# An attention, gated MLP and token-mixing kernel on one core: the written-out order of its 3395 operations is replaced by another

## The chip, the cores and the metric

One core of a Trainium2 chip runs one program. The time is the device time of one execution in microseconds (us). The engines are TensorE (PE in the profile; PEld is its loading of weights), VectorE (DVE), ScalarE (ACT), GpSimd (POOL) and SyncE (SP), and 16 DMA engines that all queues share. A DMA is issued by SP, by POOL or, at the very start, by ACT, and counts as an instruction of that queue: an issue stands in the queue behind whatever the issuing engine waits for.

## What is computed

Three blocks in a row, all float32, with 4 batches, 448 positions, 768 features (12 heads of 64):

```python
scores = cap * np.tanh(scale * (q @ k.T) / cap)          # per batch and head
attn = exp(scores) / sum(exp(scores))
x = concat_heads(attn @ v)                                # (4, 448, 768)

h = relu(x @ w_in)                                        # d_ff 1024: u | v
v_n = (v - mean) / sqrt(var + 1e-6)
v_s = einsum('ts,bsd->btd', w_spatial, v_n) + b_spatial
x = (u * v_s) @ w_out

theta = x @ w_theta
y = einsum('ts,bsd->btd', w_tok_r, x * cos(theta)) + einsum('ts,bsd->btd', w_tok_i, x * sin(theta))
u = x + y
out = u + relu(u @ w_ch)
```

The MLP weights come as 64-bit words and are turned into float32 on the chip.

## The kernel before

Most products are made three times, from the high and low parts of both factors, which are float32 values rounded to a coarser form and the differences left over. In the scores the two parts lie over each other in the partitions, so that one pass of 128 rows does two of these products.

**Attention** runs over pairs of heads. The six pairs of the first batch are "direct": their probabilities go into the product with V unsplit (`attend_1`, L833). All the rest, three batches of six pairs, splits the probabilities (`attend`). For a pair, in turn:

- SP, ACT or POOL loads Q, K and V. Pairs 0 and 1 load each Q half by itself (`load_twice` L568, the tails of 64 rows L571 and L576, `load_k` L536); the others load Q and K for two pairs at once (`load_q` L529, L536, `load_tails` L543). V of a direct pair comes by four small DMAs (`load_v1`, L619 and L621), into one of two buffers, whose ones and zeros POOL sets by five memsets at the start (`ones_1`, L462 to L466).
- PE turns Q and K (`turn`: L642 to L646 for pairs 0 and 1, L659 for others) into a PSUM tile `tqk`.
- ACT and DVE copy the high parts of Q (`y`, L683) and K (`XA` L713, `XB` L714), DVE makes the low ones (L359, the helper `difference`). POOL copies pieces of K to where each product needs them (`XT`, L719, L721, L723; `XH`, L730).
- From pair 2 on, Q's high part is needed in both halves of the partitions. This is done by DMAs from SBUF to SBUF on SP, 112 KB each: `y_odd` (L706, two DMAs) fills the tile `y1` from `y0`, then `y_even` (L709) writes the upper half of `y0` once y_odd has read it and DVE has made the low part from it. The tiles are called `y` for even and `Y` for odd pairs among the direct ones, and `yl` holds the low part.
- PE makes four groups of scores (L356, the helper `products`; one of 3 and three of 4 products), ACT takes tanh (L769) and exp (L772) of each, and PE adds up the products with V in `acc` (L356). Copies of `acc` and its row sums follow (L859, L867); a gather of the sums through DRAM (L924, L928, L935, L940) and the division end the pair.

Beside this, in the first 100 us, POOL and SP load w_in in twelve DMAs of 512 KB (`load`, L986), and POOL, ACT and DVE turn each into float32 and into high and low parts (L399 to L420, L999, L359); the turning of w_spatial (L1037 to L1062) follows.

**The rest**: v, u and the spatial mix of the MLP for each batch (`moe1_v`, `moe1_u`, `moe1_s`), the second product, theta with cos and sin, the token mix, the last product with w_ch. Attention of one batch runs between MLP work of the batch before it.

**What sets the order.** Each step is entered in a list by `op(...)` with its engine, its readers and writers, but it is emitted only at the end, in the sequence of a table of numbers, `ORDER` (L47 to L217). `Plan.order` returns the table, and the last lines of the kernel go through it:

```python
    def order(self):

        assert sorted(ORDER) == list(range(len(self.ops)))
        place = {i: n for n, i in enumerate(ORDER)}
        assert all(place[d] < place[i] for i, op in enumerate(self.ops) for d in op[4])
        return ORDER
...
    with tc.manual_schedule():
        for i in plan.order():
            plan.ops[i][3]()
```

Each engine executes its own instructions in the sequence in which they were emitted; a step waits in its queue until what it reads is there and what it overwrites is free, and everything behind it in that queue waits too.

Of the kernel before, what the change touches and what calls it, by code (L numbers as in the profile page):

```python
# [47 lines left out]
    4, 9, 10, 5, 7, 8, 2, 36, 12, 38, 3, 6, 0, 11, 31, 33, 35, 13, 1, 14, 34, 37, 32, 15, 29, 16, 195, 27, 18, 23, 20,  # L48
    30, 26, 17, 21, 56, 28, 19, 22, 39, 24, 25, 140, 70, 63, 143, 141, 142, 40, 144, 145, 57, 58, 146, 54, 52, 196,
    41, 53, 149, 147, 48, 55, 194, 45, 51, 43, 71, 148, 59, 154, 46, 42, 72, 150, 155, 64, 44, 65, 156, 47, 153, 60,  # L50
    49, 151, 66, 50, 161, 152, 198, 61, 162, 67, 77, 163, 164, 73, 62, 200, 157, 210, 202, 165, 212, 211, 74, 199,
    207, 167, 166, 197, 201, 175, 208, 159, 168, 204, 206, 170, 79, 205, 176, 203, 78, 160, 169, 236, 68, 213, 80, 84,
    158, 171, 286, 248, 209, 81, 238, 69, 177, 249, 174, 173, 237, 285, 172, 240, 82, 287, 239, 241, 217, 243, 83, 86,
    250, 214, 218, 178, 242, 215, 98, 247, 219, 244, 245, 220, 85, 180, 235, 216, 246, 87, 228, 179, 91, 221, 223, 75,
    88, 229, 76, 181, 222, 251, 289, 105, 230, 224, 89, 100, 90, 301, 291, 302, 303, 227, 290, 226, 99, 296, 293, 225,
    299, 292, 294, 182, 298, 231, 297, 101, 295, 93, 92, 252, 102, 232, 288, 255, 106, 300, 253, 331, 233, 256, 103,
    107, 258, 104, 254, 304, 183, 108, 266, 257, 119, 471, 259, 261, 472, 94, 267, 109, 260, 95, 110, 305, 126, 343,
    265, 184, 96, 268, 344, 345, 111, 121, 120, 262, 333, 234, 97, 332, 112, 122, 473, 308, 306, 338, 263, 269, 335,
    309, 340, 123, 336, 307, 264, 372, 311, 124, 310, 334, 339, 319, 271, 337, 312, 346, 125, 128, 314, 272, 270, 330,
    313, 341, 114, 373, 127, 315, 113, 129, 320, 342, 185, 318, 115, 321, 374, 130, 316, 322, 116, 376, 273, 317, 133,  # L60
    131, 347, 324, 377, 350, 348, 325, 475, 323, 353, 378, 351, 132, 354, 361, 379, 349, 478, 274, 474, 186, 352, 117,
    380, 187, 383, 188, 118, 381, 356, 275, 490, 189, 191, 492, 384, 355, 192, 190, 479, 357, 375, 193, 480, 276, 362,
    483, 491, 489, 382, 488, 134, 360, 485, 482, 358, 487, 493, 486, 363, 385, 476, 326, 386, 477, 389, 481, 327, 364,
    359, 387, 328, 390, 484, 525, 278, 329, 494, 365, 277, 526, 282, 501, 388, 495, 283, 279, 392, 496, 280, 284, 506,
    502, 366, 497, 393, 391, 281, 507, 498, 512, 527, 367, 503, 529, 528, 508, 404, 582, 394, 541, 584, 509, 504, 395,
    542, 513, 396, 543, 368, 405, 505, 499, 531, 583, 514, 406, 510, 511, 530, 539, 369, 585, 407, 500, 515, 537, 517,
    516, 534, 408, 544, 518, 520, 532, 538, 533, 540, 521, 535, 536, 135, 370, 136, 522, 397, 371, 519, 586, 545, 398,
    137, 587, 552, 546, 523, 409, 547, 399, 524, 553, 557, 138, 635, 416, 550, 554, 139, 563, 551, 558, 417, 548, 555,
    588, 410, 556, 418, 400, 600, 419, 559, 602, 601, 562, 564, 549, 560, 401, 420, 590, 565, 428, 598, 429, 589, 561,
    430, 566, 595, 431, 603, 421, 567, 593, 568, 422, 591, 571, 569, 596, 592, 594, 597, 572, 570, 599, 402, 411, 604,  # L70
    573, 636, 403, 611, 412, 605, 432, 574, 606, 616, 423, 612, 575, 609, 413, 433, 637, 617, 622, 610, 613, 638, 424,
    694, 443, 623, 414, 444, 614, 607, 445, 425, 650, 691, 446, 624, 652, 447, 615, 448, 618, 608, 692, 621, 434, 651,
    619, 449, 435, 639, 457, 620, 625, 693, 646, 450, 640, 415, 451, 436, 643, 576, 630, 626, 653, 647, 627, 642, 631,
    645, 628, 641, 648, 649, 629, 644, 452, 437, 632, 695, 654, 633, 696, 661, 426, 655, 634, 453, 656, 438, 745, 577,
    427, 666, 662, 659, 454, 667, 439, 672, 578, 657, 663, 697, 660, 668, 458, 658, 459, 709, 669, 440, 460, 664, 711,
    461, 673, 665, 455, 579, 698, 462, 674, 670, 702, 671, 456, 710, 705, 463, 677, 700, 708, 675, 712, 441, 703, 680,
    699, 676, 678, 707, 464, 701, 465, 704, 679, 706, 681, 442, 581, 713, 580, 682, 746, 796, 819, 683, 714, 720, 820,
    747, 684, 816, 821, 725, 715, 817, 721, 797, 718, 916, 798, 726, 731, 716, 719, 722, 748, 685, 732, 717, 799, 818,
    466, 800, 760, 913, 467, 723, 761, 762, 806, 727, 724, 807, 914, 808, 733, 728, 686, 730, 749, 729, 750, 756, 687,
    809, 734, 468, 915, 752, 755, 751, 739, 753, 757, 735, 758, 763, 736, 810, 740, 754, 738, 759, 688, 737, 834, 742,  # L80
    917, 469, 743, 918, 741, 764, 470, 835, 765, 966, 771, 766, 801, 769, 772, 744, 776, 770, 773, 767, 802, 689, 803,
    777, 804, 690, 782, 774, 768, 919, 778, 805, 775, 811, 931, 779, 812, 783, 933, 932, 813, 921, 814, 780, 920, 928,
    781, 784, 815, 927, 822, 787, 922, 924, 785, 929, 823, 925, 790, 825, 786, 934, 926, 828, 836, 824, 788, 826, 846,
    930, 791, 789, 827, 923, 837, 829, 792, 967, 830, 935, 793, 968, 838, 794, 936, 942, 937, 1025, 947, 940, 943,
    847, 948, 941, 848, 944, 795, 849, 938, 953, 831, 939, 945, 969, 832, 954, 946, 850, 833, 1022, 839, 981, 949,
    982, 983, 952, 840, 950, 1023, 970, 851, 841, 955, 974, 858, 980, 951, 977, 971, 859, 852, 1024, 972, 860, 956,
    978, 973, 976, 961, 975, 853, 979, 984, 842, 958, 957, 854, 861, 959, 843, 962, 960, 862, 963, 1026, 844, 985,
    1027, 964, 992, 986, 845, 965, 863, 987, 1075, 993, 997, 990, 855, 870, 864, 1003, 998, 991, 988, 856, 885, 994,
    1028, 989, 999, 871, 865, 872, 1040, 857, 1000, 873, 995, 1042, 1041, 886, 1004, 887, 996, 866, 888, 1030, 874,
    1029, 1001, 1005, 1002, 1033, 875, 1006, 1032, 1043, 1008, 1036, 1031, 1037, 876, 1038, 1007, 1011, 1034, 1009,  # L90
    889, 1010, 1039, 1012, 877, 1035, 867, 878, 1044, 868, 1013, 1076, 879, 890, 1045, 1014, 1077, 1051, 1046, 869,
    1015, 1056, 891, 1049, 1134, 1052, 899, 1057, 892, 880, 1050, 893, 1053, 1016, 1047, 1078, 881, 1058, 1062, 1132,
    1048, 1054, 894, 1059, 882, 895, 1090, 1063, 896, 1092, 1091, 897, 1060, 1064, 900, 1133, 901, 1079, 1055, 898,
    1070, 1086, 1131, 1080, 1017, 883, 1018, 1085, 1061, 1081, 1089, 1082, 1087, 1067, 1084, 1065, 1093, 1083, 884,
    1088, 902, 1066, 1068, 903, 904, 1069, 1019, 1071, 905, 1094, 1073, 1135, 1101, 1095, 1136, 1074, 1072, 906, 1102,
    1106, 1185, 1096, 1112, 1107, 1099, 1020, 907, 1097, 1103, 1137, 1100, 908, 1113, 909, 1098, 1149, 1021, 910,
    1104, 1151, 1150, 911, 1108, 1105, 1236, 1237, 1138, 1109, 1114, 1111, 1140, 1142, 1110, 1139, 1145, 1238, 912,
    1115, 1239, 1141, 1152, 1117, 1146, 1240, 1256, 1148, 1143, 1116, 1259, 1147, 1120, 1118, 1119, 1121, 1144, 1260,
    1257, 1153, 1261, 1122, 1186, 1160, 1258, 1123, 1154, 1187, 1124, 1241, 1155, 1165, 1161, 1158, 1356, 1242, 1159,
    1166, 1171, 1162, 1156, 1188, 1125, 1157, 1167, 1243, 1354, 1244, 1200, 1168, 1246, 1245, 1163, 1247, 1201, 1172,  # L100
    1202, 1248, 1164, 1249, 1189, 1251, 1126, 1353, 1173, 1169, 1199, 1170, 1127, 1190, 1250, 1355, 1193, 1191, 1197,
    1176, 1195, 1174, 1198, 1192, 1194, 1196, 1179, 1175, 1177, 1203, 1252, 1178, 1180, 1128, 1253, 1182, 1357, 1274,
    1183, 1358, 1181, 1204, 1211, 1205, 1406, 1275, 1206, 1212, 1216, 1209, 1184, 1254, 1213, 1210, 1222, 1207, 1255,
    1217, 1130, 1286, 1214, 1208, 1359, 1129, 1218, 1287, 1215, 1371, 1219, 1223, 1221, 1372, 1373, 1265, 1220, 1224,
# [2055 lines left out]
```

## Time and profile before

| | us |
|---|---|
| three runs | 777.21, 778.95, 778.85; median 778.85 |
| span of the profiled execution, first to last instruction | 777.3 |
| PE busy, 3720 matmuls | 755.6 (97%) |
| DVE busy | 607.3 (78%) |
| ACT busy | 455.3 (59%) |
| POOL busy | 306.0 (39%) |
| DMA | 59.26 MB, 76 GB/s in the mean |

The profile gives one execution with its span; a time of its own for that execution is not shown, so the span is set beside the three runs. "Busy" leaves out the time that an engine waits. In the views of waits, a name behind `<-` is what the engine waited for last. In the timeline, a row is one instruction or a run of like ones, with its start, its duration, its engine (SPq and POOLq are DMA issues, where the number is the time that the issue took, not that of the transfer), and in brackets the idle time just ahead of it.

### The profile page before, as it was taken

To read this page: it belongs to the slowest core of one execution; us is meant where nothing else is said; L and a number is where in the kernel's file an instruction comes from. 1 tells how busy PE (TensorE), PEld (TensorE's weight loads), DVE (VectorE), ACT (ScalarE), POOL (GpSimd) and SP (SyncE) were. 2 spreads that over 40 slices of the span, in tenths; PEclk is the share of its full clock that TensorE was granted. 3 is DMA by queue.
4 is the path that set the end of the run, shared out by engine and by line. 5 is a ranking of instruction groups with operands and counts; after the bars stand their busy time and mean duration, and the time that the engine had idled before them with its cause. 6 is when DMAs were issued, how large, how long until landed. Compare 5 with 4: busy or idle time off the path is not lost.

```text
span 777.3 us, 10897 instructions
## 1 busy us (share of the span) xinstructions
PE 755.6 (97%) x3720; PEld 645.6 (83%) x3720; DVE 607.3 (78%) x984; ACT 455.3 (59%) x752; POOL 306.0 (39%) x441
## 2 busy tenths in 40 slices
PE   6899999999999999999999999999999999999997
PEld 3565678888888778887799988999999999999986
DVE  3758989888866897589988767888887977987545
ACT  3888977878779778886555544432433423343333
POOL 4868775645646455661202000120200200762160
PEclk9999999999999999999999999999999999999999
DMA  6578433243242431511243420010011000011104
GB/s 190 148 200 224 104 81 81 63 120 88 52 109 63 107 92 33 130 47 42 86 147 101 132 69 21 21 42 21 22 40 41 21 22 2 0 36 36 64 20 130
DMA packets 78219, 59.26 MB, mean 76 GB/s; under 512 B 47074, under 2 KB 71364, under 8 KB 78164
## 3 DMA queue, kind: packets, MB, share of 16 engines
q1 hardware_dynamic: 76260, 54.61, 26.8%
q0 software_dynamic: 1152, 3.64, 1.3%
q8 instruction: 29, 0.48, 0.3%
q10 hardware_dynamic: 752, 0.33, 0.2%
q14 instruction: 26, 0.21, 0.1%
HBM read 44.18 MB, written 5.62 MB: 64 GB/s over the span
## 4 chain that ended last, share of the span: by engine, by line
PE 80%; DVE 8%; ACT 5%; issue 3%; POOL 2%; DMA 2%; SPq 0%; POOLq 0%; DVEq 0%; ACTq 0%
PE ps_mm L356 17%; PE y_ps L356 13%; PE th_ps L356 11%; PE f_ps L356 11%; PE acc L356 10%; PE sc L356 6%; PE ps_sum L356 3%; PE ps_av L356 3%; PE z_ps L1602 2%; PE tqk L659 1%; DVE s L943 1%; ACT e L769 1%; ACT e L772 1%; DVE ll L359 1%; ACT et L769 1%
## 5 line engine op out<-in xcount | busy, mean ns | idle before, releaser
L356 PE MATMUL y_ps<-tok_h,zt 128*128 128x448 f32 x336 | 102.7, 369 | 0.0
L1538 POOL TENSOR_SCALAR n<-n 128x448 f32<-128x448 f32 x24 | 15.4, 642 | 204.3 <-DVE n L1535 204.3
L772 ACT ACTIVATE e<-e,cap_sb 128x896 f32<-128x896 f32 x72 | 74.3, 1048 | 0.6
L769 ACT ACTIVATE e<-sc,icap 128x896 f32<-128x896 f32 x72 | 71.3, 1007 | 4.9 <-PE sc L356 4.6
L356 PEld LDWEIGHTS y_ps<-tok_h,zt 128*128 128x128 f32 x336 | 63.1, 188 | 6.2 <-DVE zt L359 0.4
L359 DVE TENSOR_TENSOR ll<-e,hh 128x896 fp32r<-128x896 f32 x54 | 61.5, 1146 | 8.0 <-ACT hh L777 6.1
L356 PE MATMUL y_ps<-tok_l,zt 128*128 128x448 f32 x168 | 61.8, 368 | 0.0
L356 PE MATMUL f_ps<-x,ch_h 128*128 128x448 f32 (+2 forms) x204 | 57.8, 365 | 0.0
L356 PE MATMUL th_ps<-x,th_ah 128*128 128x448 f32 x192 | 55.9, 372 | 0.1
L356 PE MATMUL ps_mm<-w_in_h,x 128*128 128x512 f32 (+1 forms) x132 | 49.0, 400 | 1.8 <-DVE gated L1205 1.2
L356 PE MATMUL ps_mm<-x,w_in_h 128*128 128x448 f32 x168 | 48.4, 369 | 0.4 <-ACT gated L1095 0.3
L356 PE MATMUL sc<-yl,XH 128*128 128x448 f32 x126 | 46.5, 369 | 0.0
L1607 ACT CAST zt<-z_ps 128x896 fp32r<-128x896 f32 x24 | 21.8, 907 | 42.2 <-PE z_ps L1602 26.7
L859 ACT COPY xun<-acc 64x448 f32<-64x448 f32 x48 | 25.2, 525 | 35.2 <-PE acc L356 21.9
L1559 ACT ACTIVATE z<-z,hpi 128x448 f32<-128x448 f32 x24 | 16.1, 671 | 49.5 <-DVE z L1554 49.0
L359 POOL TENSOR_TENSOR x<-x,x 128x448 fp32r<-128x448 f32 x18 | 24.4, 1362 | 43.7 <-ACT x L1508 43.7
L356 PE MATMUL acc<-ll,vh 128*128 128x448 f32 x108 | 40.0, 370 | 0.6 <-DVE ll L359 0.5
L867 DVE COPY s<-acc 1x448 f32<-1x448 f32 (+1 forms) x48 | 29.7, 619 | 13.0 <-PE acc L356 10.2
L356 PE MATMUL acc<-hh,vl 128*64 128x448 f32 x108 | 39.5, 366 | 0.0
L356 PE MATMUL acc<-hh,vh 128*128 128x448 f32 x108 | 39.5, 365 | 0.0
L356 PEld LDWEIGHTS f_ps<-x,ch_h 128*128 128x128 f32 x204 | 37.0, 188 | 2.6 <-DVE p L2033 0.2
L356 PEld LDWEIGHTS th_ps<-x,th_ah 128*128 128x128 f32 x192 | 35.0, 188 | 2.9 <-ACT x_last L1349 0.2
(306 smaller groups left out, 2273.1 us busy)
## 6 DMA issues: line engine op xcount, KB each, us to landing
y<-y SPq DMA_DIRECT2D x60, 112.0 KB
bits<-in_moe_w_ch_dram SPq DMA_DIRECT2D x12, 384.0 KB
rq<-in_q_dram SPq DMA_DIRECT2D x33, 128.0 KB
rk<-in_k_dram SPq DMA_DIRECT2D x11, 384.0 KB
r<-d SPq DMA_DIRECT2D x16, 224.0 KB
rv<-in_v_dram SPq DMA_DIRECT2D x18, 192.0 KB
w_in_bits<-in_moe_w_in_dram POOLq DMA_DIRECT2D x6, 512.0 KB, 5.3
w_in_bits<-in_moe_w_in_dram SPq DMA_DIRECT2D x6, 512.0 KB
```

The source lines that it names most:

```text
L356: nc.tensor.matmul(out=ps, lhsT=a, rhs=r, start=(first and i == 0), stop=(last and i == len(terms) - 1))
L359: (engine or nc.vector).tensor_tensor(out=o, in0=x, in1=f32(hi), op=ALU.subtract)
L659: nc.tensor.transpose(o, a, ident)
L769: nc.scalar.activation(out=st["e", g], in_=src, func=ACTF.Tanh, scale=icap)
L772: nc.scalar.activation(out=st["e", g], in_=st["e", g], func=ACTF.Exp, scale=cap_sb)
L859: (nc.scalar.copy if xe == "act" else nc.vector.tensor_copy)(out=xun[b, p][64 * hd:64 * hd + 64, :], in_=st["acc", hd][x0:x0 + 64, :])
L867: nc.vector.tensor_copy(out=st["s"][64 * hd:64 * hd + n, :], in_=st["acc", hd][64 - x0:64 - x0 + n, :])
L943: nc.vector.reciprocal(out=st["s"], in_=st["s"])
L1538: nc.gpsimd.tensor_scalar(out=st["n"], in0=st["n"], scalar1=1.0, scalar2=-MAGIC, op0=ALU.mult, op1=ALU.add)
L1559: nc.scalar.activation(out=st["z"][:, 0:S], in_=st["z"][:, 0:S], func=ACTF.Sin, scale=-1.0, bias=hpi)
L1602: nc.tensor.transpose(st["t"][:, kk * 128:(kk + 1) * 128], z["z"][:, kk * 128:(kk + 1) * 128], ident)
L1607: nc.scalar.copy(out=st["h"].rearrange("p c n -> p (c n)"), in_=st["t"][:, 0:n])
```

## The change

Only the numbers of `ORDER` change: 169 lines of the table out, others in. The list of operations is the same 3395, each on the engine that it had. Two lines of the table, as an example:

```diff
-    4, 9, 10, 5, 7, 8, 2, 36, 12, 38, 3, 6, 0, 11, 31, 33, 35, 13, 1, 14, 34, 37, 32, 15, 29, 16, 195, 27, 18, 23, 20,
...
+    9, 10, 36, 4, 7, 8, 12, 6, 5, 38, 11, 31, 33, 2, 35, 37, 0, 14, 32, 34, 15, 29, 16, 195, 27, 18, 20, 17, 56, 28,
```

In their engine's queue stand at another place: 830 of 1080 operations of PE, 774 of 911 of DVE, 520 of 705 of ACT, 296 of 404 of POOL, 147 of 230 of SP. The farthest moves are 53 places on PE and 12 on SP. Three places in detail.

**The start, on POOL.** `tt` are the tails of Q and K, `v_112` and `v_113` the two V buffers. Before, behind the first tail and most of the memsets of the first buffer:

```order
L465 MEMSET v_112 64x64
L466 MEMSET v_112 64x64
L576 DMA tt<-in_k_dram 64x2x64
L462 MEMSET v_113 128x3x64
L463 MEMSET v_113 128x3x64
L464 MEMSET v_113 128x256
L465 MEMSET v_113 64x64
L466 MEMSET v_113 64x64
L571 DMA tt<-in_q_dram 64x2x64
L730 TENSOR_SCALAR XH_95<-XA 64x256
```

Now:

```order
L571 DMA tt<-in_q_dram 64x2x64
masks.py:199 ISA
masks.py:199 AFFINE_SELECT ident<-ident 128x128
L576 DMA tt<-in_k_dram 64x2x64
L571 DMA tt<-in_q_dram 64x2x64
L462 MEMSET v_112 128x3x64
```

The three tails of pair 0 now go out ahead of all memsets; those of `v_113` come behind the pieces XT and XH of pair 0. On SP, the first Q loads of pair 0 (L568) were issued as two, then the tails of pair 1 (L571, L576), then the third; now one tail of pair 1 (L571) goes first and the three follow it together. The load of `cap` (L432) moves from the fifth place to behind K of pair 1.

**The copies of pair 2, on SP.** Before, from the V loads behind y_odd (L706) of pair 2 on:

```order
L619 DMA v_112<-in_v_dram 128x3x64
L621 DMA v_112<-in_v_dram 64x64
L924 DMA d<-s 2x448
L709 DMA y<-y 64x448
L529 DMA rq<-in_q_dram 128x4x64 x3
L536 DMA rk<-in_k_dram 128x4x192
L543 DMA tt<-in_q_dram 64x4x64
L543 DMA tt<-in_k_dram 64x4x64
L706 DMA Y<-Y 64x448 x2
```

Now:

```order
L619 DMA v_112<-in_v_dram 128x3x64
L621 DMA v_112<-in_v_dram 64x64
L709 DMA y<-y 64x448
L529 DMA rq<-in_q_dram 128x4x64 x3
L706 DMA Y<-Y 64x448 x2
L536 DMA rk<-in_k_dram 128x4x192
L543 DMA tt<-in_q_dram 64x4x64
L543 DMA tt<-in_k_dram 64x4x64
L924 DMA d<-s 2x448
```

y_even of pair 2 (L709) no longer stands behind the gather of the sums (L924), and y_odd of pair 3 (L706 on `Y`) goes ahead of the K and tail loads of pair 4. On POOL the fifth load of w_in (L986) moves by two places: before, one high part (L999) stood ahead of it since the copies of pair 2, now two do, and all pieces of XT with them.

The readers of this copy, on PE (`acc_373` and `acc_417` are the two heads' products of pair 1, `acc_392` and `acc_425` in the new numbering). Before:

```order
L659 MATMUL tqk_387<-ident_80,rk_267 128x128 x3
L356 MATMUL acc_373<-et_322,v1_113 128x448
L356 MATMUL acc_373<-e_369,v1_113 128x448
L356 MATMUL acc_417<-et_322,v1_113 128x448
L356 MATMUL acc_417<-e_369,v1_113 128x448
L356 MATMUL sc_436<-y_338,XA_91 128x448
```

Now:

```order
L659 MATMUL tqk_379<-ident_80,rk_245 128x128 x3
L356 MATMUL acc_392<-e_333,v1_113 128x448 x2
L356 MATMUL acc_392<-et_318,v1_113 128x448
L356 MATMUL acc_392<-e_376,v1_113 128x448
L356 MATMUL sc_419<-y_339,XA_91 128x448
L356 MATMUL sc_419<-yl_345,XH0_95 128x448
```

Here the first two products of pair 1 with V (`x2`) come behind the turn, where before they came ahead of it, and the first four scores of pair 2 stand ahead of the second head's products (two matmuls on `acc_417` before, `acc_425` now), which follow behind them.

Further on on SP, y_even of pair 4 (L709) stands directly behind a load of w_in (L986), which follows the four V loads of pair 3; before, it stood behind y_odd of its own pair, a gather step (L928) and four V loads. y_even of pair 3 stands behind a gather (L924), as before, but no longer behind a load of w_in and four V loads that came between.

**The first pair of the second batch, on POOL.** `vh` and `vl` are the high and low parts of V, which split pairs need. Before:

```order
L730 TENSOR_SCALAR XH_95<-XA 64x256
L607 TENSOR_SCALAR vh<-rv 128x8x64
L359 TENSOR_TENSOR vl<-rv,vh 128x512
L721 CAST XT<-XA 128x64
L503 DMA x_tail<-x 128x2x64
L603 MEMSET vh 128x8x64
```

Now:

```order
L721 CAST XT<-XA 128x64
L359 TENSOR_TENSOR w_in_l<-w_in_f,w_in_h 128x512
L719 CAST XT<-XA 64x64
L723 CAST XT<-XB 64x64
L730 TENSOR_SCALAR XH_95<-XA 64x256
L730 TENSOR_SCALAR XH_96<-XB 64x256
L730 TENSOR_SCALAR XH_96<-XA 64x128
L603 MEMSET vh 128x8x64
L607 TENSOR_SCALAR vh<-rv 128x8x64
L359 TENSOR_TENSOR vl<-rv,vh 128x512
```

The copy XT at L721 moves from behind `vh` and `vl` to ahead of them; one `w_in_l` difference now stands between the pieces of K.

## Rows read from the trace of the kernel before

**Rows 1.** The page's head and its first part: busy time of each engine.

```profile
span 777.3 us, 10897 instructions
PE 755.6 (97%) x3720; PEld 645.6 (83%) x3720; DVE 607.3 (78%) x984; ACT 455.3 (59%) x752; POOL 306.0 (39%) x441
```

**Rows 2.** Busy time by windows of 20 us: length, PE, PEld, DVE, ACT, POOL, clock, DMA.

```profile
0.00:20.00 20.00, 13.38 (x43) 7.95 (x44) 8.30 (x23) 7.56 (x11) 9.70 (x33) 1.00 0.70 191
20.00:40.00 20.00, 17.80 (x69) 11.72 (x68) 14.54 (x23) 16.29 (x23) 16.29 (x30) 0.97 0.60 153
40.00:60.00 20.00, 19.59 (x73) 12.53 (x73) 12.66 (x20) 17.64 (x26) 13.78 (x21) 0.94 0.76 204
60.00:80.00 20.00, 18.78 (x70) 11.29 (x70) 16.79 (x21) 17.75 (x28) 15.87 (x26) 1.00 0.72 193
80.00:100.00 20.00, 18.16 (x77) 12.43 (x76) 18.60 (x27) 18.41 (x28) 16.39 (x22) 1.00 0.52 129
100.00:120.00 20.00, 20.00 (x97) 16.49 (x97) 16.33 (x24) 13.81 (x21) 13.66 (x24) 1.00 0.21 52
```

**Rows 3.** PE's waits: line and releaser, us in total, times, longest.

```profile
PE tqk L642 <- DMA rq<-in_q_dram: 3.3, 1, 3.3
PE sc L356 <- POOL XT L721: 2.2, 2, 1.1
PE sc L356 <- DMA y<-y: 2.2, 1, 2.2
```

**Rows 4.** Timeline of the start.

```profile
3.48 0.61 SPq L568 DMA_DIRECT2D rq<-in_q_dram  x1
...
5.21 0.58 POOL L571 DMA_DIRECT2D tt<-in_q_dram  x1
...
6.35 0.87 PE L642 MATMUL tqk<-ident,rq 128*128 128x128 f32 x3 [3.28 <-DMA rq<-in_q_dram]
...
7.75 0.34 PE L643 MATMUL tqk<-ident,tt 64*128 64x64 f32 x1 [0.53 <-DMA tt<-in_q_dram]
...
12.00 0.74 PE L356 MATMUL sc<-y,XT 128*128 128x448 f32 x1 [1.10 <-POOL XT L721]
...
15.68 0.84 PE L642 MATMUL tqk<-ident,rq 128*128 128x128 f32 x3
```

**Rows 5.** Timeline around the copies of pair 2.

```profile
27.90 1.16 SPq L706 DMA_DIRECT2D y<-y  x2
...
32.08 0.62 SPq L621 DMA_DIRECT2D v<-in_v_dram  x1
...
32.49 0.61 POOL L986 DMA_DIRECT2D w_in_bits<-in_moe_w_in_dram  x1
...
33.50 0.51 SPq L709 DMA_DIRECT2D y<-y  x1
...
34.92 0.92 PE L356 MATMUL acc<-e,v 128*128 128x448 f32 x2
...
38.03 0.44 PE L356 MATMUL sc<-y,XA 128*128 128x448 f32 x1 [2.19 <-DMA y<-y]
```

**Rows 6.** The chain of waits, 0 to 100 us: start, us, what.

```profile
33.50 4.39 DMA y<-y
```

**Rows 7.** DMA issues on POOL's queue: count, KB each, median us from issue to landing.

```profile
w_in_bits<-in_moe_w_in_dram POOLq DMA_DIRECT2D x6, 512.0 KB, 5.3
x_tail<-x POOLq DMA_DIRECT2D x6, 64.0 KB, 2.0
```

**Rows 8.** The window right after the wait of pair 2, columns as in rows 2.

```profile
38.90:42.20 3.30, 3.30 (x7) 2.00 (x7) 0.00 (x0) 2.90 (x4) 2.92 (x6) 0.50 1.07 261
```

**Rows 9.** Timeline around the first scores of the second batch.

```profile
84.49 1.63 POOL L359 TENSOR_TENSOR vl<-rv,vh 128x512 fp32r<-128x512 f32 x1
...
86.07 1.93 POOL L721 CAST XT<-XA 128x64 fp32r<-128x64 f32 x1
...
88.06 0.47 PE L356 MATMUL sc<-y,XT 128*128 128x448 f32 x1 [1.15 <-POOL XT L721]
```

336 rows, old and new, of the table ORDER are left out of this document.

## The prediction, made before the changed kernel was run

> **What bounds the kernel now.** I read the page's first part first: PE is busy 755.6 of 777.3 us [rows 1]. The operations and their durations stay, so an order can win only at the 21.7 us in which PE is idle, and at stretches where it works at a lower clock. The busy time by windows tells where these are: from 0 to 100 us PE is busy 13.38, 17.80, 19.59, 18.78 and 18.16 of 20 each, 12.3 us idle; from 100 to 120 it is 20.00 [rows 2]. More than half of all idle time lies in the first eighth, where ACT runs at 16 to 18 of 20, the DMA engines at 0.5 to 0.8, and POOL at 14 to 16. PE's waits name the pieces: 3.3 us for the first Q load, 2.2 for y_even of one pair, twice 1.1 for XT [rows 3]. The lower clock shows in the window of 38.90 to 42.20: granted 0.50, so 1.2 instead of 2.4 GHz, right after PE stood for 2.19 us [rows 5, 8].
>
> From 100 us on nearly every matmul follows the one before, so what PE gains before that should reach the end, and moves after it are worth little. 830 moved places on PE count as nothing where PE is full: the sum of its matmuls is the same in any order.
>
> **Term 1, the start.** The turning of pair 0 begins at 6.35, when Q's third load, issued on SP at 3.48, has landed: 2.87 us from issue to matmul [rows 4]. Now that load has one tail of pair 1 and two loads ahead of it, not two tails and two loads. One issue is worth 0.6 to 0.7 us (0.61 in the row), so the turning begins about 0.7 earlier, at 5.65. The tail of POOL that PE waited another 0.53 us for was issued at 5.21 and read at 7.75, 2.54 us later [rows 4]; without five memsets and the second buffer's five ahead of it, it goes out about 2 us earlier, and its wait disappears. That is 1.2 at the end of the turning. The next hand-off, 1.10 us for XT [rows 4], I take to change little: the groups of scores change places so that XA and XH come first, which takes XT off the path but puts XH on it, made by the same engine POOL right behind its w_in issue. I give it 0.2. The second turning then starts at about 14.3 instead of 15.68: **−1.4**. Bounds: −0.7 (only the load) and −2.3 (0.7 + 0.53 + 1.10).
>
> **Term 2, y_even of pair 2.** It was issued at 33.50, behind the gather that waited for DVE, and landed 4.39 us later [rows 5, 6]; PE stood from 35.84 (34.92 + 0.92) to 38.03. In the new order it stands right behind the four V loads. y_odd comes about 1.3 us earlier (term 1), so at 26.6; from there the V loads follow as before, which took 4.8 us from 27.90 to 32.70 (32.08 + 0.62) with an internal wait. So y_even is issued between 30.4 and 31.4. How long does it take? In the trace I have 64 KB in 2.0 and 512 KB in 5.3 us on POOL's queue [rows 7]; in a straight line between them 112 KB take 2.35, an estimate from these rows. The upper bound is the 4.39 of the same copy, issued 1 us behind a load of w_in on POOL [rows 5, 6]. I take 2.35, since that load now stands further behind in POOL's queue. Landing: 32.8 to 33.8, against PE, which arrives at 35.84 − 1.4 (term 1) − 1.5 (the two heads' products that now come behind; four matmuls by 0.37) = 32.9. A wait of 0 to 0.9 remains, 0.3 in the middle: **−1.9**. With 4.39 us it would be 34.8 to 35.8 and a wait of 1.9 to 2.9: a gain of 0.3 or a loss of 0.7.
>
> The Trainium skill, page "DMA: Bandwidth & Descriptors", section "Anatomy of one DMA — SWDGE (gpsimd) path", gives 2.0 us plus the bytes by 436 GB/s, which would be an estimated 2.26 us here and a term of −2.0 in place of −1.9. The same page speaks against the change under "Queues, rings and completion order": each DMA engine goes round between the queue rows that it has work for. By that, a place in SP's queue buys nothing while a load of POOL's queue is under way, and the term would be near nothing if w_in's load starts as early as before. The rows agree as far as they go: 4.39 us with the load under way.
>
> **Term 3, the clock.** The 3.30 us at 0.50 [rows 8] did half the work that they do at full clock. If PE no longer stands for 2 us ahead of them, 1.65 us come back: **−1.7**. Bounds: 0 if a wait of this size stays (at this place or the next), 1.7 if not. The two go together.
>
> **Term 4, XT of the second batch.** POOL made vl (84.49 to 86.12) and only then XT, until 88.00; PE stood 1.15 us [rows 9]. XT now goes ahead of vh and vl: **−1.1**. What comes in its place are vh and vl themselves, read only by the products with V several microseconds later, and one w_in difference, about 1.3 us of POOL. Bounds: −1.15 and 0, the latter if the difference delays the last K piece as much.
>
> **Term 5, what takes up the slack.** PE now runs 5 us earlier from 40 us on, against ACT, which was busy 53.8 of the 60 us from 40 to 100 [rows 2]: 6.2 us of room in all. PE's own idle time there is 3.47 (60 less 19.59, 18.78, 18.16); 1.15 is term 4's. Of the remaining 2.3, made by ACT and DVE chains, I expect half again on top: **+1.2**. Bounds: 0, and all 5 us.
>
> Edits that I cost at nothing: `cap` later on SP (read by DVE only for the tanh, long after the turning); V of pair 1 later on POOL (memsets of `v_113`, read 10 us on); the tails of x on POOL (2.0 us to landing [rows 7], read by the MLP's v many us later); all moves from 100 us on, whose cover is PE's full queue (20.00 of 20); if it broke, each hole costs its own length, under 1 us each in the waits of before.
>
> **The sum** −1.4 −1.9 −1.7 −1.1 +1.2 = −4.9 us, so 772.4 against the profiled span of 777.3. The median of the three runs, 778.85, lies 1.55 above that span; I carry this over: **773.95, about 774.0**.
>
> **Rivals.** A difference under 0.3% (2.3 us, 776.5 to 781.2) is about what a measurement of this kernel can't tell from no change.
>
> *One late copy.* y_even at pair 2 still meets the w_in load, or y_even of pair 3 does (its scores now come right behind the turning of pair 4). The wait of 2.2 and the slow stretch of 1.7 come back once: −4.9 + 3.9 = −1.0, 777.9. For it speaks the busy share of the DMA engines, 0.76 between 40 and 60 us [rows 2]; against it, that the copy leaves SP 2 to 3 us earlier. By the Trainium skill's rule on the queue rows (page "DMA: Bandwidth & Descriptors", above) this case is the likelier one wherever a load of w_in is under way. *The slack is used up.* ACT binds from 40 to 100 us and the first 5 us are lost there: only term 4 stays, 777.75. Against it are the 6.2 us of room. Together 0.23.
>
> *Slower: two late copies.* y_even of pair 4 now stands directly behind a w_in load on SP, y_even of pair 3 lands about when PE arrives. It decides when both copies take over 4.4 us, the time of the late one here [rows 6], or when the load ahead waits for its buffer: then each costs 2.2 + 1.7, and −4.9 + 7.8 = +2.9 gives 781.7. Chance 0.14. That the change does not do what it says is not a rival of size: the queues show the moves; their effect beyond 100 us may be nil, which is in the forecast.
>
> **How the numbers follow.** The forecast has 0.63, with a range of its own of 771.5 to 776.5 (at best terms 1 to 4 at full, −2.3 −2.2 −1.7 −1.15 = −7.35, 771.5; at worst the bound of no difference). With the "same" cases and half of the slower one the range of 8 in 10 is 771.0 to 780.0: the half microsecond below is for holes that close in the rest of the kernel. So faster by over 0.3%: 0.63; within: 0.23; slower: 0.14.
>
> **What would show it.** The waits of PE: Q's first load about 2.6 instead of 3.3, the tail gone, y<-y below 0.5, XT at most 1.1. Between 30 and 45 us the clock stays at 1.00, and PE's busy time from 20 to 40 rises from 17.80 to over 19. The matmul of the second turning begins near 14.3. I am wrong if y<-y stands in the waits with 2 us or more (with the clock at 0.50 behind it), if ACT's e leads the waits between 40 and 100 us, or if the window of 100 to 120 shows PE far from 20.00.

## The result and the profile after

The changed kernel took 785.11 us in the median (784.43 to 787.72, 4 runs) against 778.36: ratio 1.0092, 95% interval 1.0072 to 1.0112. It is **slower by 6.75 us**, where 774.0 was forecast, and outside the range of 771 to 780. The page of its profiled execution:

```profile
span 785.6 us, 10939 instructions
...
PE 757.5 (96%) x3720; PEld 645.8 (82%) x3720; DVE 607.5 (77%) x984; ACT 454.5 (58%) x752; POOL 294.1 (37%) x441
```

PE's idle time went from 21.7 [rows 1] to 28.1 us, and its busy time rose by 1.9 for the same 3720 matmuls. The windows, with the columns of [rows 2]:

```profile
0.00:20.00 20.00, 14.05 (x47) 8.80 (x48) 7.79 (x22) 7.24 (x10) 9.81 (x33) 1.00 0.67 184
20.00:40.00 20.00, 19.28 (x77) 12.52 (x76) 13.46 (x20) 18.50 (x28) 15.61 (x27) 1.00 0.63 171
...
80.00:100.00 20.00, 18.34 (x81) 13.17 (x82) 19.01 (x28) 16.94 (x28) 13.54 (x20) 1.00 0.50 129
100.00:120.00 20.00, 18.41 (x88) 14.68 (x87) 15.96 (x25) 13.88 (x21) 16.19 (x26) 1.00 0.36 78
...
160.00:180.00 20.00, 17.89 (x83) 15.41 (x82) 14.60 (x19) 13.81 (x19) 9.48 (x13) 0.91 0.41 95
...
680.00:740.00 60.00, 57.37 (x300) 51.78 (x299) 41.70 (x67) 18.73 (x46) 27.55 (x25) 1.00 0.11 35
```

The first two windows gained, as forecast (PE 33.3 busy of 40 against 31.2). But 100 to 120, 160 to 180 and 680 to 740, where PE was full before, have holes now. The same two late windows of before:

```profile
160.00:180.00 20.00, 20.00 (x101) 17.19 (x100) 18.93 (x23) 15.14 (x23) 11.95 (x19) 1.00 0.47 115
...
680.00:740.00 60.00, 60.00 (x321) 55.51 (x320) 43.53 (x75) 21.86 (x54) 22.44 (x20) 1.00 0.14 47
```

PE's waits name them (columns of [rows 3]):

```profile
PE sc L356 <- DMA y<-y: 6.7, 8, 2.1
PE tqk L642 <- DMA rq<-in_q_dram: 3.0, 1, 3.0
PE z_ps L1602 <- DVE z L1567: 1.8, 1, 1.8
PE sc L356 <- DVE yl L359: 1.3, 1, 1.3
```

The one wait for y<-y of 2.2 us [rows 3] is gone. Eight others came, all behind 100 us: 1.49 at 102, 0.77 at 146.6, 2.11 at 165, 0.65 at 232, 0.34 at 249, 0.90 at 264, and two of 0.2. With the scores that come late, ACT is late too: 0.67 for its et at 251. To follow the loss I read from each trace when the 300th, 500th, ... of the 3720 matmuls starts, and subtract the start in the trace of before. The columns on the right are experiments, named below:

| matmul | before, us | after | start_new_3 | two_parts | one_spread | end_old | both_mended |
|---|---|---|---|---|---|---|---|
| 300 | 93.6 | −3.1 | −3.3 | +0.2 | −1.6 | −2.9 | −3.8 |
| 500 | 135.8 | −1.3 | −0.5 | −0.3 | −1.6 | −1.4 | −2.5 |
| 700 | 175.0 | +3.2 | −0.6 | −0.3 | +1.4 | +1.6 | −0.2 |
| 1200 | 277.4 | +6.3 | −0.7 | −0.3 | +1.3 | +5.9 | +2.0 |
| 3000 | 638.0 | +4.4 | −1.1 | −0.3 | +1.5 | +2.8 | −1.4 |
| 3600 | 752.6 | +7.7 | −1.1 | −0.2 | +1.5 | +2.8 | −1.4 |

So the kernel was 3.1 us ahead at 90 us, had lost 9.4 by 284, and lost 3.3 more about 683 and 728. A lag carries run-to-run chance of 1 to 2 us: the same instructions up to 150 us stand at 0 in before and at −1.6 in one_spread, mostly because the clock fell in one and not in the other (last section). And where PE's sequence differs, the nth matmul is not the same one. The medians of the runs decide, and since before itself ran at 777.3 to 778.4 beside the different runs, a kernel is compared with another by its ratio to the before of its own runs.

**One of the waits, in both lists.** Pair 5 of the second batch, before (timeline):

```profile
157.60 0.56 SPq L536 DMA_DIRECT2D rk<-in_k_dram  x1
...
158.21 1.15 SPq L706 DMA_DIRECT2D y<-y  x2
...
163.21 0.56 SPq L709 DMA_DIRECT2D y<-y  x1
...
164.65 1.23 SPq L940 DMA_DIRECT2D r<-d  x2
...
165.90 0.44 PE L356 MATMUL sc<-y,XT 128*128 128x448 f32 x1
```

and after:

```profile
157.02 1.27 SPq L940 DMA_DIRECT2D r<-d  x2
...
158.34 0.59 SPq L536 DMA_DIRECT2D rk<-in_k_dram  x1
...
159.03 1.14 SPq L706 DMA_DIRECT2D y<-y  x2
...
161.60 0.65 SPq L503 DMA_DIRECT2D x_tail<-x  x1
...
164.81 0.51 SPq L709 DMA_DIRECT2D y<-y  x1
...
167.16 0.44 PE L356 MATMUL sc<-y,XT 128*128 128x448 f32 x1 [2.11 <-DMA y<-y]
```

The spreading of the row sums (L940, two DMAs of 224 KB) stood behind y_even; now it stands ahead of K's load and y_odd. y_odd is issued 0.8 us later, and y_even, which has to wait for its landing, 5.78 us behind it instead of 5.00: 1.6 later in all. PE's list asks for the scores 0.85 us earlier (165.05, where the wait begins, against 165.90), and the 2.11 us are there. Then the clock fell as well (window, columns of [rows 2]):

```profile
168.40:171.40 3.00, 3.00 (x10) 2.65 (x9) 1.05 (x2) 2.94 (x4) 2.27 (x3) 0.50 0.58 132
```

The same chain was pulled ahead for pairs 4 (second batch), 3 and 5 (third batch), three of the other places with a wait.

### The profile page after: what moved, and what is told of

It reads as the page before. It is cut to its first block, busy times and chain, and to the rows that moved or that the text cites. A ratio compares the mean times of both kernels' runs of the same rounds, so it can differ in the third digit from the quotient of the medians.

```text
span 785.6 us, 10939 instructions
## 1 busy us (share of the span) xinstructions
PE 757.5 (96%) x3720; PEld 645.8 (82%) x3720; DVE 607.5 (77%) x984; ACT 454.5 (58%) x752; POOL 294.1 (37%) x441
## 4 chain that ended last, share of the span: by engine, by line
PE 44%; DVE 4%; DMA 1%; ACT 1%; issue 0%; SPq 0%; DVEq 0%; ACTq 0%
PE y_ps L356 13%; PE th_ps L356 11%; PE f_ps L356 8%; PE ps_mm L356 4%; PE z_ps L1602 2%; PE ps_av L356 2%; PE ps_sum L356 2%; DVE s_f L1822 1%; PE tok_ps L1447 1%; DVE S L1831 0%; DMA bits<-in_moe_w_theta_dram 0%; PE o_ps L1702 0%; PE o_ps L1996 0%; DMA out_dram<-o_tail 0%; DVE x L359 0%; DVE p L1979 0%
## 5 line engine op out<-in xcount | busy, mean ns | idle before, releaser
L356 PE MATMUL y_ps<-tok_h,zt 128*128 128x448 f32 x336 | 107.5, 371 | 0.0
L356 PE MATMUL ps_mm<-w_in_h,x 128*128 128x512 f32 (+1 forms) x132 | 47.3, 396 | 0.3 <-DVE w_sp_l L359 0.3
L796 POOL TENSOR_SCALAR et_hl<-et 64x448 fp32r<-64x448 f32 x36 | 27.5, 764 | 32.3 <-ACT et L772 10.3
L402 ACT ACTIVATE hb<-bits 128x384 f32<-128x384 f32 (+4 forms) x40 | 22.7, 567 | 28.2 <-DMA bits<-in_moe_w_ch_dram 8.5
```

The costliest lines, as they stand in the source:

```text
L356: nc.tensor.matmul(out=ps, lhsT=a, rhs=r, start=(first and i == 0), stop=(last and i == len(terms) - 1))
L402: nc.scalar.activation(out=hb(), in_=f32(words()[:, :, 1]), func=ACTF.Copy, scale=2.0 ** -112)
L796: nc.gpsimd.tensor_scalar(out=st["t", hd][r, :], in0=st["e", 0][r, :], scalar1=1.0, scalar2=0.0, op0=ALU.mult, op1=ALU.add)
```

## The experiments

Theory A says that SP's new sequence does it. Its rivals: B, that an early PE runs into late copies with any list; C and D, that the copies' own places or PE's earlier asking do it; and that the last third is only a consequence. All kernels below compute the whole result.

**The two lists put together, new start.** The diff, with `new` and `old` for the two tables:

```diff
-ORDER = new
+ORDER = new[:390] + [i for i in old if i not in new[:390]]
```

> The first 390 operations of the new list (all that runs up to about 90 us), then the rest in the sequence of before. The changed kernel is 3.1 us ahead of before at the 300th matmul (90.5 instead of 93.6 us) and loses it all later. Theory A (the later queue of SP loses it: copies between the q halves are put behind the spreading of the sums and other loads): the lead is kept but for what later waits take of it, 778.4 - 3.1 + about 1 = 776, faster than both. Rival B (PE being early is what makes the later copies late, whatever the list): the lead is lost, 778 to 779.

Measured: 782.15 against 777.29, ratio 1.0054 (1.0036 to 1.0072). Not what either theory said: PE stood 4.96 us at 87 us for `w_sp_l` of DVE. The new list has this step ahead of two scalings (L946), the seam put it behind them, and they waited for their sums (the kernel is one line longer):

```profile
88.66 2.73 DVE L947 TENSOR_TENSOR xun<-xun,r 128x448 f32<-128x448 f32 x2 [0.40 <-DMA r<-d]
...
91.31 0.61 DVE L360 TENSOR_TENSOR w_sp_l<-w_sp_ps,w_sp_h 128x448 fp32r<-128x448 f32 x1
...
91.98 0.80 PE L357 MATMUL ps_mm<-w_in_h,x 128*128 128x512 f32 x1 [4.96 <-DVE w_sp_l L360]
```

Only ACT stood for the late load of w_in that an expectation below names. Behind that the lag stayed at +2.9 from matmul 500 to 1400: the old rest loses nothing.

**The reverse.**

```diff
+ORDER = old[:390] + [i for i in new if i not in old[:390]]
```

> The reverse: the first 390 operations of before, then the rest in the new sequence. Theory A: the later list costs by itself, what the changed kernel lost after its lead (from -3.1 at matmul 300 to +7.6 at 3500, so 10.7) less what came from being early (up to 1.5, the wait at 102 us): 778.4 + 9 to 10.7 = 787.5 to 789. Rival B: PE is later, the copies are in time, and it comes out at or below the changed kernel: 783 to 785.

787.22 against 777.29, ratio 1.0123 (1.0098 to 1.0148): +9.9. The late waits are there without an early start (2.40 at 164, 1.28 at 250, 1.42 at 263.6, 1.77 at 682). **The new list costs by itself from 90 us on**; B falls as the account of the loss.

**The spreading behind y_even.** On SP alone, four times as here for pair 5:

```diff
 L935 DMA d_1676<-c 128x14
-L940 DMA r<-d_1676 64x2x448 x2
 L536 DMA rk<-in_k_dram 128x4x192
 L706 DMA y<-y 64x448 x2
 L543 DMA tt<-in_q_dram 64x4x64
 L543 DMA tt<-in_k_dram 64x4x64
 L503 DMA x_tail<-x 128x2x64
 L709 DMA y<-y 64x448
+L940 DMA r<-d_1676 64x2x448 x2
```

> The new list with four steps moved on SP alone: the spreading of the sums (two DMAs of 224 KB, L940) of pairs 1 and 3 in the second and third batch stands behind y_even of the pair that it was put ahead of. Every other engine keeps its new sequence. Theory A: the waits for y<-y at 146.6, 165.1, 232.1 and 264.0 us (0.77 + 2.11 + 0.65 + 0.90 = 4.4) go, and with the second one the half clock from 168.3 to 171.5 (1.6): 785.1 - 6 = 779. Rival C (the copies are late because y_odd and y_even themselves stand later, or because PE asks earlier): at most 1 us is won, 784 to 785.

791.37, ratio 1.0169 (1.0146 to 1.0192): 14 us slower than before, and wrong by theory A too. The timeline at the same place shows why:

```profile
157.25 1.14 SPq L706 DMA_DIRECT2D y<-y  x2
...
160.67 0.51 SPq L709 DMA_DIRECT2D y<-y  x1
...
161.23 1.24 SPq L940 DMA_DIRECT2D r<-d  x2
...
165.97 0.62 DVE L946 TENSOR_TENSOR xun<-xun,r 128x448 f32<-128x448 f32 x1 [2.60 <-DMA r<-d]
...
168.53 0.47 PE L356 MATMUL sc<-y,XA 128*128 128x448 f32 x1 [3.18 <-ACT et L769]
```

The copies are in time: y_even goes out 3.4 us behind y_odd, not 5.8, and the first scores start at 163.16 without a wait. But the new list had put the scaling that reads the sums (L946) forward on DVE as well. DVE now stands 2.60 us for it, a copy behind it (L867) is late, ACT with it, and PE stands 3.18 us for ACT. That part of A is shown (what stands ahead of the copies on SP makes them late), and C falls with it; that moving it back is enough is refuted.

**The scaling moved back too**: L946 of these pairs, with what reads it, at its old place on DVE (and two steps on ACT), besides the edit above.

```diff
-L946 TENSOR_TENSOR xun<-xun,r 128x448
 L867 COPY s<-acc 64x448
 L943 RECIPROCAL s<-s 128x448
...
+L946 TENSOR_TENSOR xun<-xun,r 128x448
```

> The run with the spreading of the sums put behind y_even removed the waits for y<-y at 165 us (y_odd took 2.2 us again, not 5.2), but DVE then stood 2.60 us for the spread sums in the scaling step (L946), with a copy behind it that ACT and PE waited for: 3.18, 2.9 and 2.5 us in place of 2.1, 0.65 and 0.9. Here that scaling (L946 of pairs 1 and 3 of the second and third batch, with the steps that read it) also goes back to its place of before. Theory A (spread and scaling were pulled ahead together; one of them pinches the copies, the other DVE): both kinds of waits go, 785.1 - 4 to -6 = 779 to 781. Rival D (PE asks for the scores 2 us earlier behind their turning, and something of the chain is always too late then): the waits appear at the next step, 784 or more.

783.83, ratio 1.0078 (1.0057 to 1.0098) against 1.0092: 1.1 us below the changed kernel, with intervals that overlap, where 4 to 6 were expected. The number is nearer to D's 784 than to A's 779 to 781. The waits at 146, 165, 232 and 264 are gone; 1.27 at 103 and 1.07 at 245 stay, and new ones for DVE's `gated` (L1205), 1.72 at 171.7 and 0.77 at 267, take back part of what was won:

```profile
PE ps_mm L356 <- DVE gated L1205: 2.5, 2, 1.7
```

In the list of before one chain costs more than this (below).

**The scores as late on PE as before**, for four pairs, for example pair 4, whose first scores now come behind eleven products with V and three others:

```diff
...
+L356 MATMUL ps_mm<-w_sp_h,vn_h 128x448
+L356 MATMUL ps_mm<-w_sp_l,vn_h 128x448
+L356 MATMUL ps_mm<-w_sp_h,vn_l 128x448
 L356 MATMUL sc<-y,XT 128x448
 L356 MATMUL sc<-y,XB 128x448
 L356 MATMUL sc<-yl,XT 128x448
```

> The new list with PE's sequence changed at four places alone: the first scores of pairs 4 and 5 of the second and third batch stand as far behind the turning of their Q and K as before (9.5, 10.4, 9.3, 10.4 us of PE work by the planner's own costs, instead of 6.9, 8.2, 7.8, 8.8). SP and all other engines keep the new sequence. Theory D (PE asks too early): the waits at 146.6, 165.1, 248 to 251 and 264 (0.77 + 2.11 + 0.34 + 0.67 + 0.90 = 4.8) shrink to below 1 and the half clock at 168 (1.6) goes: 779 to 780. Theory A (SP's queue): the copies come as late as they do, but PE asks 1.5 to 2.6 us later: the same fall where the wait is below that. So both say a fall; if it stays at 784 or more, what stands between turning and scores is not the cause, and the delay moves on to ACT, which gets its scores later.

786.91, ratio 1.0124 (1.0101 to 1.0146). The waits for y<-y at 146 and 165 go, and PE stands for ACT's e instead (0.89 at 158.6, 0.51 at 173.5) and for `gated` (0.48 at 177). D falls as the account of the loss: a pair's whole chain is late, and asking later only moves the wait to its next link.

**The reverse in the list of before**: the four chains of sums pulled ahead, and then only that of pair 3 of the second batch (below), which meets the copies of pair 5. The small inversion on DVE (L931) that lies in a chain moves with it.

```diff
+L928 DMA c<-d 128x14
 L549 DMA rv<-in_v_dram 128x2x192
 L552 DMA rv<-in_v_dram 64x2x64 x2
-L928 DMA c<-d 128x14
+L935 DMA d_1680<-c 128x14
+L940 DMA r<-d_1680 64x2x448 x2
 L503 DMA x_tail<-x 128x2x64
 L536 DMA rk<-in_k_dram 128x4x192
 L706 DMA y<-y 64x448 x2
```

> The list of before with the spreading of the sums of pairs 1 and 3 (second and third batch), and the small steps that it needs, moved ahead of y_odd of pairs 4, 5, 3 and 5 on SP (and one small step on DVE), as in the new list; PE, ACT and POOL as before. Theory A: y_odd takes 3.5 to 5 us instead of 2.3 to 4.3 and y_even lands later; the copies had 1.8, 0.1, 1.0 and 1.3 us to spare there, so waits of 0 to 1, 2, 1 and 1 us appear: 777.8 + 2 to 4 = 780 to 782. Theory D (without PE asking earlier it costs nothing): 778.

> The list of before with one chain moved, that of pair 3 of the second batch: gather, inversion and spreading of its sums (two DMAs of 224 KB, L940) go ahead of y_odd of pair 5. Theory A: one wait of about 2.1 us at 165, and 1.6 more where the clock falls behind it: 777.3 + 2.1 to 3.7 = 779.4 to 781. If the four chains only act together, or the small step on DVE is what costs: below 778.5.

Four chains: 783.10 against 777.33, ratio 1.0070 (1.0048 to 1.0093). One: 781.26 against 777.48, ratio 1.0054 (1.0034 to 1.0073), **3.8 us by one chain of DMAs and one small DVE step**, which were not moved apart. Timeline of the latter:

```profile
156.75 1.23 SPq L940 DMA_DIRECT2D r<-d  x2
...
159.46 1.22 SPq L706 DMA_DIRECT2D y<-y  x2
...
165.15 0.51 SPq L709 DMA_DIRECT2D y<-y  x1
...
167.45 0.44 PE L356 MATMUL sc<-y,XT 128*128 128x448 f32 x1 [2.02 <-DMA y<-y]
```

PE's sequence is that of before here, and the wait of 2 us is there; with 0.68 us at 156 for `gated`, this trace lost 2.9 us between matmul 500 and 700 and nothing behind that. So the chain ahead of the copies is enough to make the wait, without PE asking earlier.

**The end.**

```diff
+ORDER = new[:2200] + [i for i in old if i not in new[:2200]]
```

> The first 2200 operations of the new list (to about 475 us), the rest as before. The lag of the changed kernel grows from +4.6 us at matmul 2100 to +7.6 at 3600, with one wait of 1.78 us for DVE at 683 us and one of 0.74 at 728. If the list of the last third costs this by itself: 785.1 - 3.0 = 782. If it is a matter of being late from before: 785, no change.

781.18, ratio 1.0055 (1.0035 to 1.0074): 0.37% or 2.9 us below the changed kernel, as expected (3.9 by the bare medians). A place in the changed kernel (DVE's timeline):

```profile
672.51 0.93 DVE L1546 SCALAR_TENSOR_TENSOR r<-n,r 128x448 f32<-128x448 f32 x1
...
676.11 1.09 DVE L359 TENSOR_TENSOR zt<-z_ps,zt 128x896 fp32r<-128x896 f32 x1 [2.67 <-ACT zt L1607]
...
677.65 0.39 DVE L1550 TENSOR_SCALAR r<-r 128x448 f32<-128x448 f32 x1
...
678.42 0.62 DVE L1554 SCALAR_TENSOR_TENSOR z<-r 128x448 f32<-128x448 f32 x1
...
680.26 1.37 DVE L1822 TENSOR_TENSOR s_f<-ch_h 128x384 f32<-128x384 f32 x1
...
684.42 0.61 DVE L1567 TENSOR_TENSOR z<-z,x_last 128x448 f32<-128x448 f32 x1
```

Two short steps that PE's next turning of z needs (L1550, L1554) stand behind a low part for which DVE waits 2.67 us, and sums (L1822) that nobody needs yet stand ahead of the last product (L1567). Undone at this one place:

```diff
 L1546 SCALAR_TENSOR_TENSOR r<-n,r 128x448
+L1550 TENSOR_SCALAR r<-r 128x448
+L1554 SCALAR_TENSOR_TENSOR z<-r 128x448
 L359 TENSOR_TENSOR zt<-z_ps,zt 128x896
...
 L1567 TENSOR_TENSOR z<-z,x_last 128x448
+L1822 TENSOR_TENSOR s_f<-ch_h 128x384 x2
```

> The new list with DVE's sequence changed at one place: two short steps of the last theta tile (clamp L1550 and size L1554, 0.39 and 0.62 us) go ahead of a low part (L359) for which DVE stood 2.67 us at 673.4, and two sums (L1822) behind the products that the turning of z waits for. If this place makes the wait of 1.78 us at 683 (of the 3 us that the list of the last third costs): ratio to before 1.0092 - 1.8/777 = 1.007, 783. If the wait comes of being late overall: 785.

784.65, ratio 1.0081 (1.0060 to 1.0102). In its trace the wait at 683 is gone (the lag moves by 0.05 from matmul 3000 to 3300, in the changed kernel by 2.4). The medians, 0.5 apart with intervals that overlap, don't tell the gain.

**Both mended.** The spreading and scaling as above, and the old list from the 2201st operation on.

> The new list with both mends: spreading and scaling of the four pairs back behind y_even (783.8 by itself), and the operations from the 2201st on in the sequence of before (781.2 by itself). If they are two separate causes they add up: 785.1 - 1.3 - 3.9 = 780. If the end's loss comes of the lag that the attention made, the second adds nothing to the first: 783.

779.76, ratio 1.0030 (1.0015 to 1.0044): the two are separate and add up within the intervals (0.14% and 0.37% off the 1.0092 give 1.0041); the 783 of one cause, a ratio of 1.007, is out.

**For a faster list.** First the new start with the seam mended (all that either list has among its first 390), then with the seam at 115 us (535, as shown) and three loads moved on SP (the last w_in load forward, K and V of pair 2 behind y_even of pair 1):

```diff
+first = set(new[:535]) | set(old[:535])
+ORDER = [i for i in new if i in first] + [i for i in old if i not in first]
```

> As the first of these runs (new list to about 90 us, then that of before), but the seam mended: there a load of w_in (with its conversion) fell behind the seam and PE stood 4.96 us for it at 87.0. Now all that either list has among its first 390 operations comes first, in the new sequence. Theory A: the lead of 3.1 us at matmul 300 (plus up to 0.5) is kept by the old rest, which lost nothing after the seam in that run (2.91 at matmul 800 and 2.84 at 1400): 777.8 - 2 to -3 = 775. Rival B (an early PE runs into late copies with any list): 777 to 779.

> A last try for a faster list: the first 535 operations of either list (to about 115 us) in the new sequence, the rest as before, so that the seam lies behind the first pairs of the second batch; and on SP the last load of w_in goes ahead of two V loads, and K and V of pair 2 go behind y_even of pair 1, since that copy took 4.74 us among these loads and PE stood 1.49 us at 102 us. Theory A: the lead of 3.1 us at matmul 300 stays, 777.3 - 2 to -3 = 774.5 to 775.5. Rival B (an early start always meets a late copy or a weight that is converted late): no gain, 777 to 779.

The first met the same wait again, 3.68 us at 85 us for the same `w_sp_l` behind the two scalings: 781.40, ratio 1.0057 (1.0035 to 1.0078). The second has no such wait: 778.52, ratio 1.0010 (0.9999 to 1.0021), no gain. It is 3.3 us ahead at matmul 300, 1.1 at 400 and 0.5 at 500. Last, terms 2 and 4 alone in the list of before:

```diff
+L709 DMA y<-y 64x448
 L924 DMA d<-s 2x448
-L709 DMA y<-y 64x448
...
+L721 CAST XT<-XA 128x64
 L607 TENSOR_SCALAR vh<-rv 128x8x64
 L359 TENSOR_TENSOR vl<-rv,vh 128x512
-L721 CAST XT<-XA 128x64
```

> The list of before with terms 2 and 4 of the prediction alone: y_even of pair 2 ahead of the gather on SP, and the copy XT (L721) of the first pair of the second batch ahead of vh and vl on POOL. The prediction's account: the wait of 2.19 at 35.8 shrinks to 0 to 1.3 and that of 1.15 at 86.9 goes: 777.4 - 2 = 775.5. If what PE gains in the first 100 us is lost again between 90 and 115 us, as in the run with the new start and the seam at 115 us (-3.3 at matmul 300, -0.6 at 500), where other engines set the time: 777, no change.

778.81, ratio 1.0006 (0.9993 to 1.0018). Its waits up to 120 us:

```profile
PE ps_mm L356 <- DVE w_sp_l L359: 1.8, 1, 1.8
PE sc L356 <- DMA y<-y: 1.2, 1, 1.2
...
PE sc L356 <- POOL XT L721: 1.1, 1, 1.1
```

y<-y is down from 2.2 to 1.2 and the second XT wait gone, as forecast. In their place PE stands 1.82 us at 86 for `w_sp_l`, the step of DVE that stopped the two new starts: in the list of before it stands behind the two scalings. These took 0.61 us each in before, and take 1.02 and 1.69 here, while POOL makes vh and vl:

```profile
84.74 2.64 DVE L946 TENSOR_TENSOR xun<-xun,r 128x448 f32<-128x448 f32 x2
...
85.38 1.52 POOL L359 TENSOR_TENSOR vl<-rv,vh 128x512 fp32r<-128x512 f32 x1
```

Why they take longer was not tested. So no list here beats that of before.

## Why the prediction was wrong

**The step that failed** is "all moves from 100 us on, whose cover is PE's full queue (20.00 of 20); if it broke, each hole costs its own length, under 1 us each in the waits of before". A window with PE at 20.00 tells that every operand came in time, not by how much. Pair 5's scores started at 165.90 with y_even issued at 163.21: 2.69 us, little more than the copy itself takes. The new order of SP and DVE broke that cover at eight copies and at one turning of z, with holes of up to 2.11 us. In trace lags that made 9.4 us between 90 and 284 us (the waits of PE there and the half clock, less the waits of before, make 8.2 of them) and 3.3 at the end. That it is the list from 90 us on, and not the early start, rest_new shows: +9.9 us with the old start. I had read SP's new order as far as pair 4 of the first batch; the spreading pulled ahead of y_odd stands in the same listing further down.

**The slower rival had a late y_even right, but not its place, and its cause only once.** It named pairs 3 and 4 of the first batch, which had no wait for y<-y, and copies of over 4.4 us behind a load of w_in. Such a copy came at pair 1 of the second batch, read 4.87 us behind its issue:

```profile
94.27 0.58 SPq L986 DMA_DIRECT2D w_in_bits<-in_moe_w_in_dram  x1
...
98.94 0.51 SPq L709 DMA_DIRECT2D y<-y  x1
...
103.81 0.44 PE L356 MATMUL sc<-y,XT 128*128 128x448 f32 x1 [1.49 <-DMA y<-y]
```

In start_new_3, where the load of w_in goes ahead and K and V go behind the copy, PE has no wait for it. At 165 us, though, y_even itself took no longer than usual; it was issued late, since y_odd had been held up by the spreading, which the rival does not name. The half clock behind the wait came as it says. I gave it 0.14, for the two places alone. Two of the prediction's own signs of being wrong came with it: a wait for y<-y of 2 us with the clock at 0.50 behind it, and 18.41 of 20 from 100 to 120 us.

**Term 1** (−1.4): the second turning starts at 14.91 instead of 15.68, −0.8. The tail's wait went (0.53); the first load's fell by 0.26, not 0.7; XT's 1.10 became 0.51 for XA and 1.25 for yl. **Term 2** (−1.9): right in the trace, issue at 31.18 (30.4 to 31.4 was forecast) and no wait; but PE came for the copy at 34.02, not at 32.9, so a copy of up to 2.84 us would have done.

```profile
14.91 0.84 PE L642 MATMUL tqk<-ident,rq 128*128 128x128 f32 x3
...
31.18 0.48 SPq L709 DMA_DIRECT2D y<-y  x1
...
34.02 0.71 PE L356 MATMUL sc<-y,XA 128*128 128x448 f32 x1
```

**Term 3** (−1.7): the clock stayed at 1.00 there, as forecast, but this was no gain to count: see below. **Term 4** (−1.1): XT's wait went, but with term 2 in two_parts it was worth nothing. **Term 5** (+1.2) was far too small. The lead of 3.1 at matmul 300 was 0.64 at 400, with the wait of 1.49 at 102 us in between, and in start_new_3, which has no such wait and where the old list follows, 3.3 became 0.5 by matmul 500. So the rival "the slack is used up" gives the first 100 us their right end: they gained next to nothing. That it is ACT, as it says, is half of it: in the changed kernel PE waited most for ACT between 40 and 100 us (0.97, 0.93 and 0.76), but in two_parts for DVE, which was busy 18.60 of 20 in [rows 2] from 80 to 100. And the prediction's premise that operations keep their durations does not hold for DVE's L946 in two_parts.

**How the loss divides.** By the ratios, of the 0.92% the end is 0.37%, 2.9 us (end_old), the spreading with its scaling 0.14 to 0.25%, 1.1 to 1.9 us (spread_scale; both_mended against end_old), and 0.30%, 2.3 us, stay in both_mended. Each of these ratios has an interval of 0.15 to 0.2% to either side: the end's share is clear of it, that of the spreading alone in the new list is not. In both_mended's trace PE waits 2.27 us for `gated` at 170 us, 1.28 for y<-y at 244 and 0.99 at 102; which moves on DVE make `gated` late was not tried, nor was what else in the last third makes up the end's share. These causes stay open.

## What to carry to other kernels

A full engine is no cover until its margins are known: for each operand that comes by a DMA, read issue, usual time to landing, and reader, and treat every move on that queue or ahead of the reader as able to break it. Where a list is remade as a whole, look at all repeats of a pattern (here the 22 pairs with y copies), not at the places with waits now. And a step pulled forward brings its readers: undone on one queue only, it stalls the next engine, as the 791 us of spread_behind show.

## What was not expected of the hardware

- **The half clock after a wait comes in some executions and not in others.** With the same list up to 475 us, the granted clock fell to 0.50 behind a wait of 2.11 us at 165 in the changed kernel, and stayed at 1.00 behind one of 2.21 in end_old. It fell behind 1.82 us in two_parts (89.2 to 92.2) and stayed behind 2.02 in one_spread. Of the 65 executions of before that were timed beside the experiments, the 21 with a mean granted clock of 1.000 have spans of 773.9 to 776.8 us, and the 14 with 0.997 or less 776.4 to 778.1. So the 1.65 us of [rows 8] belong to that one execution, and a term taken from them should have been a chance.
- **Behind others on its queue a short copy comes microseconds late.** y_even of pair 5 took 2.35 us from issue (164.81) to its reader (167.16), when the loads ahead of it had landed. y_odd, issued at 159.03 behind 448 KB of spreading and 384 KB of K on the same queue, held y_even back until 164.81, 5.78 us; in spread_behind, without the spreading ahead, the same step took 3.42. The Trainium skill (page "DMA: Bandwidth & Descriptors", section "Anatomy of one DMA — SWDGE (gpsimd) path") would give an estimated 2.26 us for 112 KB, by a fit for DMAs that GpSimd issues. The 2.35 of this copy on SP's queue agrees with it; the 5.78 do not.
- **Profiled executions aren't the median.** Where both are shown, a profiled run's time stands 1.8 to 2.2 us above its span (782.36 and 780.4 in start_new, 781.77 and 779.7 in theta_early). The span of 785.6 belongs to the slowest of the changed kernel's four runs, 787.72, and by the same difference 777.3 would belong to about 779.2, an estimate: the spans are 8.3 apart, the medians 6.75.
